# Layer with banded attention and eight routed experts: the first expert's last slots listed on chip by 0/1 products, roots in pairs, shorter groups of products, and an earlier release of chunk 3's table writes

## The chip, the cores and the metric

One Trainium2 chip, one core. The metric is device microseconds of one execution; the kernel before is given as the median of three runs, and one more execution was profiled. TensorE (PE) does the matrix products, VectorE (DVE) and ScalarE (ACT) work on what they leave in PSUM, GpSimd (POOL) does elementwise work and issues indirect DMAs (gathers, scatters), SyncE (SP) issues the plain DMAs. Each engine runs its own queue strictly in order.

## The reference, cut to what matters

2048 tokens of 512 numbers, 32 heads of 16, a band of 256 keys, and 8 experts of inner width 1376 of which each token takes two.

```python
def _A_ref(x, wqkv, wo):
    qkv = (x @ wqkv).reshape(B, S, 3, H, Dh).transpose(2, 0, 3, 1, 4)
    scores = jnp.einsum("bhqd,bhkd->bhqk", q, k) * (Dh ** -0.5)
    scores = jnp.where(mask, scores, -1e9)          # 0 <= query - key < 256
    o = jnp.einsum("bhqk,bhkd->bhqd", softmax(scores), v)
    return o.transpose(0, 2, 1, 3).reshape(B, S, D) @ wo

def _B_ref(x, wg, w1, w2):
    gates = _softmax(xt @ wg)
    topk_idx = jnp.argsort(-gates, -1)[:, :2]       # two experts per token, weights renormalised
    h = _gelu(jnp.einsum("nd,edf->nef", xt, w1))
    y = jnp.einsum("nef,efd->ned", h, w2)
    return jnp.einsum("ne,ned->nd", cw, y)

h = x + _A_ref(_layernorm(x), A_wqkv, A_wo)
return h + _B_ref(_layernorm(h), B_wg, B_w1, B_w2)
```

## The kernel before, in words

All products are made of three reduced-precision products, (high, high), (high, low), (low, high), so each operand is first split into two parts: ACT writes the high part, DVE or POOL subtracts to get the low one (`split`, L474).

The tokens go through attention in four chunks of 512 (chunk index c = 0 to 3, the fourth called the last here). A chunk has eight units of four heads; unit u = 8c + g. A unit's queries and keys go through DRAM into a layout of their own, `maxes` takes row maxima, and `attend` (L757) works on key tiles A, B, C, D: scores on PE, mask, exponential on ACT, then the product with V into the one PSUM tile `oT` (L835), four such V products for each unit of the last chunk. From unit 29 on (`LATE_MASKS`) the mask is put on the scores by DVE (L755) instead of POOL. ACT copies `oT` to `o_sb` (L850) and SP writes it to DRAM.

`project(c)` (L860) reads a chunk's attention output back (`fill`), multiplies by the inverse row sums (`part`, L905 on DVE or L903 on POOL), splits, and multiplies by the output weights (L913, twelve products of 512 columns for each block of 128 tokens). For the last chunk the inner dimension comes in three steps: heads 0 to 15 (k = 0, 1), 16 to 23 (k = 2), and 24 to 31 (k = 3), the last with its reciprocals on DVE (L947). Then come row statistics (L972), the root on POOL (`rstd`, L483, one call for each block), the normalisation (L988), the write of the normalised rows to DRAM (`xnd`), transposes on PE (L998), a copy by ACT (L1000) into the single buffer `nt_t`, and the gate products (L1005).

`route` (L1016) picks two experts for each token, finds each token's slot in its expert's list by a running count (products with 0/1 matrices, L1071 to L1076), and POOL scatters (token number, gate weight) into a DRAM `table`, one indirect DMA for each block and choice (L1102): eight for chunk index 2, eight for the last chunk in two lots of four. The eight of chunk index 2 each wait for one of the V products of units 29 and 30.

`experts` (L1172) runs eight experts. The first is expert number 0, whose slots 0 to 383 (three tiles, "early") can only hold tokens of the first three chunks, since the last chunk's tokens are put from slot 384 on (`EARLY`). Its table rows come in two reads: early ones after chunk index 2's scatters, the last two tiles (slots 384 to 597, "late") after all scatters. Token rows are gathered by POOL (L1316), transposed on PE (L1321), split; the up products are L1348 (12 in one task: 384 columns for the early tiles, 214 for the late ones), the activation L1356/L1362, the down products L1380 (33 for each tile of 128 tokens), the scaling L1391, and the result is added to the output by an indirect DMA (L1403). The other experts are taken in order of size, which `rank_experts` finds after all routing; weights come by L1209 (w1) and L1211 (w2).

The order on each engine is fixed when the kernel is built: every piece of work is a task with a priority, and a planner (`Plan.order`) simulates the engines with its own durations, giving each engine the ready task of lowest priority number. So the diff changes tasks, their dependencies and priorities, and the order of instructions follows from that.

## Time and profile before

| | us |
|---|---|
| three runs | 1045.19, 1047.86, 1051.26 |
| median | 1047.86 |
| the profiled execution, its own time | 1044.5 |
| its span, first to last instruction | 1042.4 |
| PE busy in the span | 1016.8 (98%) |

The profile page gives busy time for each engine and the share of the span; a timeline lists merged stretches of one engine with the start, the length, the line, the operation with its tiles, the count, and in brackets the idle time before it with what ended it. A windows view gives for each stretch its length, then busy time and count of PE, PEld (weight loads), DVE, ACT and POOL, then the granted TensorE clock as a share of 2.4 GHz, the DMA share and GB/s.

### The profile page before, as it was taken

How to read it: one execution, taken by the hardware profiler on the slowest of the kernel's cores; microseconds unless marked ns; L12 is line 12 of the kernel's file. 1: busy time of each engine (PE TensorE's matmuls, PEld its weight loads, DVE VectorE, ACT ScalarE, POOL GpSimd, SP SyncE). 2: the span in 40 equal slices, each digit the busy share in tenths (PEclk: the TensorE clock that was granted, in tenths of full speed). 3: DMA queues.
4: the chain of work that ended last, by engine and by line, in shares of the span. 5: the costliest groups of instructions: out<-in, count | busy, mean ns of one | idle time of the engine just before them, and what ended most of it. 6: DMA issues, size and time to landing. Idle time of an engine off the chain costs nothing. (4 is left out here: it accounts for less than half of the span.)

```text
span 1042.4 us, 19919 instructions
## 1 busy us (share of the span) xinstructions
PE 1016.8 (98%) x6722; PEld 842.0 (81%) x6722; DVE 645.6 (62%) x1951; ACT 536.9 (52%) x1143; POOL 623.3 (60%) x986
## 2 busy tenths in 40 slices
PE   8999999999999999998898999999999999999997
PEld 5877777877777777754887898998999989878795
DVE  8888876887677777787752556345453554544440
ACT  3487747575766656577631555163462543525340
POOL 5687749777887958758495144186483763834111
PEclk9999999999999999999998999999999999999999
DMA  6999877768696978764516344264444544454522
GB/s 214 291 249 240 250 190 214 224 179 202 191 251 164 200 159 210 201 167 110 190 49 148 97 141 113 63 153 111 115 97 128 157 94 105 123 139 151 124 77 29
DMA packets 143887, 164.48 MB, mean 158 GB/s; under 512 B 68587, under 2 KB 86571, under 8 KB 143776
## 3 DMA queue, kind: packets, MB, share of 16 engines
q1 hardware_dynamic: 128448, 145.96, 50.3%
q0 software_dynamic: 15328, 17.16, 9.9%
q8 instruction: 55, 0.90, 0.4%
q14 instruction: 56, 0.46, 0.2%
HBM read 111.10 MB, written 51.43 MB: 156 GB/s over the span
## 5 line engine op out<-in xcount | busy, mean ns | idle before, releaser
L735 DVE CUSTOM_DVE_ANT_0 one<-one,masked 128x320 f32<-128x320 f32 (+4 forms) x512 | 230.3, 494 | 57.9 <-PE one L730 55.0
L1348 PE MATMUL one<-mr 128*128 128x288 f32 (+14 forms) x1716 | 255.9, 310 | 1.3 <-ACT mr L476 0.7
L1348 PEld LDWEIGHTS one<-mr 128*128 128x128 f32 (+1 forms) x1716 | 244.5, 187 | 10.1 <-ACT mr L476 0.9
L785 ACT ACTIVATE zone<-one 128x384 f32<-128x384 f32 (+1 forms) x480 | 208.6, 495 | 80.1 <-PE one L779 60.6
L811 POOL TENSOR_SCALAR_AFFINE_SELECT zone<-zone 128x256 f32<-128x256 f32 (+1 forms) x332 | 151.1, 479 | 61.2 <-ACT zone L785 59.4
L1380 PE MATMUL one<-zone,mr 128*128 128x512 f32 (+4 forms) x648 | 154.9, 394 | 0.0
L480 POOL TENSOR_TENSOR mr<-mf,mr 128x512 fp32r<-128x512 f32 (+4 forms) x99 | 123.8, 1262 | 41.7 <-ACT mr L476 39.9
L1380 PEld LDWEIGHTS one<-zone,mr 128*128 128x128 f32 (+4 forms) x648 | 117.0, 182 | 31.4
L779 PE MATMUL one<-mr 98*128 98x384 f32 (+1 forms) x592 | 138.5, 327 | 3.1 <-ACT zone L785 1.9
L476 ACT CAST mr<-mf 128x512 fp32r<-128x512 f32 (+6 forms) x152 | 108.3, 734 | 46.0 <-DMA mf<-in_A_wqk_dram 15.3
L779 PEld LDWEIGHTS one<-mr 98*128 98x128 f32 x592 | 96.0, 190 | 42.9 <-ACT zone L785 14.1
L730 PE MATMUL one<-mr 96*128 96x320 f32 (+4 forms) x512 | 122.8, 315 | 1.5 <-DVE mx L735 0.9
L1287 POOL DMA_INDIRECT mf<-xnd,mf x94 | 106.4, 1132 | 28.8 <-issue 26.9
L1403 POOL DMA_INDIRECT out_dram<-mf,tb x24 | 41.5, 1730 | 130.6 <-DVE mf L1391 116.4
L478 DVE TENSOR_TENSOR mr<-one,mr 128x512 fp32r<-128x512 f32 (+16 forms) x161 | 79.1, 509 | 58.3 <-ACT mr L476 58.0
L1362 ACT ACTIVATE one<-one 128x288 f32<-128x288 f32 (+13 forms) x132 | 54.7, 415 | 104.1 <-PE one L1348 103.2
L661 PE MATMUL one<-mr 128*128 128x512 f32 (+1 forms) x396 | 103.7, 389 | 3.0 <-ACT mr L476 2.8
L730 PEld LDWEIGHTS one<-mr 96*128 96x128 f32 x512 | 87.7, 190 | 22.2 <-DVE mx L735 11.6
L1403 POOL DMA_INDIRECT out_dram<-mf x40 | 65.9, 1648 | 65.6 <-DVE mf L1433 57.1
L835 PE MATMUL oT<-zone 128*17 128x384 f32 (+2 forms) x1408 | 95.7, 389 | 0.1
L476 ACT CAST mr<-one 128x512 fp32r<-128x512 f32 (+16 forms) x161 | 70.6, 448 | 31.5 <-PE one L1321 17.3
L476 ACT CAST zone<-mf 128x512 fp32r<-128x512 f32 x72 | 42.1, 620 | 78.0 <-PE one L1423 48.5
(189 smaller groups left out, 1282.9 us busy)
## 6 DMA issues: line engine op xcount, KB each, us to landing
mf<-in_B_w_dram SPq DMA_DIRECT2D x32, 688.0 KB
mf<-in_B_w_dram SPq DMA_DIRECT2D x40, 512.0 KB
qkd<-mr SPq DMA_DIRECT2D x29, 512.0 KB
mr<-qkd SPq DMA_DIRECT2D x128, 96.0 KB
mr<-qkd SPq DMA_DIRECT2D x32, 384.0 KB
mf<-in_A_x_dram SPq DMA_DIRECT2D x32, 256.0 KB
mf<-in_A_wqk_dram SPq DMA_DIRECT2D x32, 256.0 KB
qkd<-mr SPq DMA_DIRECT2D x64, 128.0 KB
```

Of the source, the lines that this page charges most:

```text
L476: a = add("ACT", 51 + n * 0.86, lambda: nc.scalar.copy(dst_h(), src()), deps, prio, bufs)
L480: b = add("POOL", 60 + n * 2.3, lambda: nc.gpsimd.tensor_sub(dst_l(), src(), f32(dst_h())), [a], prio, bufs)
L661: nc.tensor.matmul(single[bk.h][:, s], wt()[:, int(i == 1), k * 128:(k + 1) * 128], xt[:, k, s], start=(i == 0 and k == 0), stop=(i == 2 a ...
L730: nc.tensor.matmul(view()[:, j], q_of(slot)[0:96, h + j, b].rearrange("p e q -> p (e q)"), K[slot.h][0:96, h + j, (b + k0) * 64:(b + 5) * ...
L735: nc.vector.tensor_tensor_reduce(v, v, masked[:, 320 - n:], scale=1.0, scalar=NEG, op0=OP.add, op1=OP.max, accum_out=mx_t[slot.h][:, h + j ...
L779: nc.tensor.matmul(single[bk.h][:, off:off + w], K[slot.h][0:98, h // 2, r * 128:(r + 1) * 128], q_of(slot)[0:98, h // 2, 2 * b:2 * b + 2 ...
L785: return add("ACT", 51 + n * 0.833, lambda: nc.scalar.activation(dst(), single[bk.h][:, 0:n].rearrange(order, **({"e": 2, "q": 64} if "e" ...
L811: nc.gpsimd.affine_select(v, v, pattern=[[0, v.shape[1]], [-1 if far else 1, 128]], compare_op=OP.is_gt if far else OP.is_ge, fill=0.0, ba ...
L1287: nc.gpsimd.indirect_dma_start(out=xg_t[i][:, t * 128:(t + 1) * 128], out_offset=None, in_=xnd4, in_offset=bass.IndirectOffsetOnAxis(ap=ql ...
L1348: nc.tensor.matmul(bank(), a[:, k, f * 128:f * 128 + w], spot[b][:, k, c0:c1], start=(i == 0), stop=(i == 11))
L1380: nc.tensor.matmul(single[bk.h][:n], h[a][:w], spot["w2"][2 * f + b][:w], start=(f == 0 and q == 0), stop=(f == NF - 1 and q == 2))
L1403: d = nc.gpsimd.indirect_dma_start(in_offset=None, compute_op=OP.add, **kw)
```

## The change

Seven edits, all between the last units of attention and the end of the first expert.

1. The first expert's table rows are read once, all five tiles, before the last chunk's scatters; the late tiles' entries are then only those of the earlier chunks. For the last chunk, DVE compares each token's slot number with a row of numbers 385 to 640 (`find`, 0/1 matrix of 128 tokens by 256 slots for each block), and PE multiplies these by (token number, weight) (`pick_late`, L1156, four products of two columns for each pair of blocks). DVE merges the result with the read rows (`merge`, L1536 to L1538), and the late tiles are gathered from that.
2. The scatters of the last chunk now wait for that read; the second lot of four waits for the late gathers. The ranking of the experts waits for the merge.
3. The eight scatters of chunk index 2 wait for V products of units 28 and 29.
4. The last chunk's roots are taken for two blocks at a time, and the copies of the transposed rows alternate between two buffers (`nt2`).
5. The first expert's up products are three tasks of four instead of one of twelve, and its down products one task for each 128 of the inner width instead of four tasks.
6. The low parts of the first expert's w2 are all made by DVE (before: POOL from f = 3 on).
7. In `part`, a block's split waits (in the plan) for the previous step's split of the same block; the k = 2 and k = 3 reads are planned after the use of the k = 0, 1 buffers.

```diff
+F0_PRIO, X0 = 8.0 * NC + 8.0, -8.2
...
-            ins = fill(3, o3, s3, 0, 512, last, last, p - 0.3, slot)
+            ins = fill(3, o3, s3, 0, 512, last + before_, last + before_, p - 0.3, slot)
...
+                if b % 2:
+                    b0 = b - 1
+                    root = rstd(lambda b0=b0: mv_t[0][:, b0:b0 + 2, 1], lambda b0=b0: ry_t[0][:, b0:b0 + 2], seen[-2:], pb + 0.4, 2)
...
-            tb, bk = Buf("nt"), Buf("one")
+            tb, bk = Buf("nt2" if end and b % 2 else "nt"), Buf("one")
...
+        def find():
+            pos = single[bk.h][:, 0:nb * E].rearrange("p (b e) -> p b e", e=E)
+            Vv.tensor_add(t["u"], pos, over(e_pos))
+            Vv.scalar_tensor_tensor(late_v[:, b0:b0 + nb], t["u"][:, :, 0], 1.0, t["m"][:, :, 0], op0=OP.add, op1=OP.mult)
+            for b in range(nb):
+                Vv.tensor_scalar(late_p[b], late_no, late_v[:, b0 + b:b0 + b + 1], None, op0=OP.is_equal)
+
+        def pick_late():
+            ps = single[hot[1].h][:, 0:4].rearrange("p (i q) -> p i q", q=2)
+            for b in range(nb):
+                for i in range(2):
+                    nc.tensor.matmul(ps[:, i], late_p[b][:, i * 128:(i + 1) * 128], late_r[:, b0 + b], start=(b0 + b + i == 0), stop=(b0 + b == 3),
+                                     skip_group_check=True)
...
-        for t, run in zip(route_done[NC - 2], pv_runs[8 * NC - 3] + pv_runs[8 * NC - 2]):
+        for t, run in zip(route_done[NC - 2], pv_runs[8 * NC - 4] + pv_runs[8 * NC - 3]):
...
-                                 src, dd, lo="POOL" if e == 0 and f >= 3 else "DVE"))
+                                 src, dd))
...
-            a = add("POOL", 950, g, [looked] + place, prio - 1.5, extra=2600)
+            a = add("POOL", 950, g, [looked] + place + (all_xn if e == 0 and not early else []), prio - 1.5, extra=2600)
             if e == 0 and not early:
                 late_rows.append(a)
+                for t in route_done[NC - 1][4:]:
+                    plan.after(t, [a])
...
+                    for i, (a, b) in enumerate(((w1h, "xh"), (w1l, "xh"), (w1h, "xl"))):
+                        def mm4(i=i, a=a, b=b, c0=c0, c1=c1, bank=bank):
...
-            for f0, f1 in ((0, 4), (4, 8), (8, 10), (10, NF)):
+            for f0, f1 in [(f, f + 1) for f in range(NF)] if e == 0 else ((0, 4), (4, 8), (8, 10), (10, NF)):
...
-                f1 = fetch(0, b - 8, all_routes + all_xn, EARLY // 128, nt)
+                f0 = fetch(0, F0_PRIO, sum((route_done[c] for c in range(NC - 1)), []) + [xn_done[i] for i in range(4 * NC - 4)], 0, nt)
+                for t in route_done[NC - 1]:
+                    plan.after(t, [f0])
+                old = add("DVE", 100, lambda: nc.vector.tensor_copy(late_t, tb0[:, :, 0]), [f0] + hot[:1], b - 10)
+
+                def merge():
+                    ps = single[hot[1].h][:, 0:4].rearrange("p (i q) -> p i q", q=2)
+                    nc.vector.tensor_tensor(late_t, late_t, ps[:, :, 0], op=OP.max)
+                    nc.vector.tensor_copy(tb0[:, :, 0], late_t)
+                    nc.vector.tensor_add(tb0.bitcast(F32)[:, :, 1], tb0.bitcast(F32)[:, :, 1], ps[:, :, 1])
+                f1 = add("DVE", 550, merge, [old] + hot[2:], 36, [hot[1]])
+                plan.after(sort, [f1])
```

What the planner makes of it is shown at three places. The first is PE's queue at the end of attention; the rows of `oT` with 17x128 and 17x256 that are the last of their kind are unit 31's last V product, the rows on `ident` are the transposes of the early token tiles, and `one_75`, `one_74` or `one_77`, `one_78`, `one_80` hold the four blocks' output projection. Before:

```order
L835 MATMUL oT<-zone 17x128 x4
L835 MATMUL oT<-zone 17x256 x4
L1321 MATMUL one_79<-ident,mf 128x128 x4
L1321 MATMUL one_74<-ident,mf 128x128 x4
L913 MATMUL one_75<-mr 128x512 x3
L913 MATMUL one_77<-mr 128x512 x3
L913 MATMUL one_80<-mr 128x512 x3
L913 MATMUL one_78<-mr 128x512 x3
L1321 MATMUL one_76<-ident,mf 128x128 x4
L1348 MATMUL one_79<-mr 128x384 x12
L1348 MATMUL one_74<-mr 128x384 x12
L913 MATMUL one_75<-mr 128x512 x2
```

And the same place in the changed kernel's queue of PE, where L841, L1385, L925 and L1424 are the lines that were L835, L1321, L913 and L1348:

```order
L925 MATMUL one_78<-mr 128x512 x3
L925 MATMUL one_80<-mr 128x512 x3
L1385 MATMUL one_76<-ident,mf 128x128 x4
L841 MATMUL oT<-zone 17x128 x4
L841 MATMUL oT<-zone 17x256 x4
L1424 MATMUL one_77<-mr 128x384 x12
L1424 MATMUL one_79<-mr 128x384 x12
L1424 MATMUL one_76<-mr 128x384 x12
L1424 MATMUL one_77<-mr 128x384 x12
L1424 MATMUL one_79<-mr 128x384 x12
L1424 MATMUL one_76<-mr 128x384 x8
L925 MATMUL one_75<-mr 128x512 x2
```

The three transposes and the twelve k = 2 products stand ahead of the last V product now, and between that and the first k = 3 product there are 68 up products where there were 24 up products and everything else.

The second place is PE's queue from the down products to the late tiles' up products. Before (L1266 is a lookup product for the second expert, the tiles with 128x86 and the 128x128 before it are the late ones, the next two are the second expert's):

```order
L1380 MATMUL one_77<-zone_5885,mr 128x512 x12
L1266 MATMUL one_74<-rm,pick 128x20 x2
L1321 MATMUL one_76<-ident,mf 128x128 x4
L1380 MATMUL one_77<-zone_5885,mr 128x512 x3
L1380 MATMUL one_77<-mr 128x512 x3
L1321 MATMUL one_75<-ident,mf 128x86 x4
L1321 MATMUL one_78<-ident,mf 128x128 x4
L1380 MATMUL one_77<-mr 128x512 x3
L1321 MATMUL one_80<-ident,mf 128x128 x4
L1348 MATMUL one_79<-mr 128x214 x12
```

In the changed kernel, where L1156 is the new product of the 0/1 matrices and L1455 the down products:

```order
L1455 MATMUL one_78<-zone_5928,mr 128x512 x12
L1156 MATMUL one_77<-mf 128x2 x4
L1455 MATMUL one_78<-zone_5928,mr 128x512 x12
L1455 MATMUL one_78<-mr 128x512 x6
L1455 MATMUL one_80<-zone_5928,mr 128x512 x6
L1385 MATMUL one_79<-ident,mf 128x128 x4
L1385 MATMUL one_76<-ident,mf 128x86 x4
L1455 MATMUL one_80<-zone_5928,mr 128x512 x12
L1424 MATMUL one_75<-mr 128x214 x12
```

Between the second list product and the late transposes stand 24 down products; 15 down products of the third early tile are left for after the late tiles' up products, as are the second expert's transposes.

The third place is POOL's queue around the late gathers, of which the second has 86 rows. Before, all scatters (L1102) come first:

```order
L1102 DMA table<-ent_6257,si_6290 18432x2
L1101 MEMSET spacer 1x1
L1102 DMA table<-ent_6257,si_6290 18432x2
L480 TENSOR_TENSOR mr<-mf,mr 128x384 x2
L480 TENSOR_TENSOR mr<-mf,mr 96x384
L1316 DMA mf<-xnd,tb_147 128x512
L1316 DMA mf<-xnd,tb_147 86x512
L1316 DMA mf<-xnd,tb_148 128x512 x3
```

In the changed kernel (L1161 the scatters, L1478 the adding of an early tile's result to the output, L1380 the gathers):

```order
L1161 DMA table<-ent_6200,si_6249 18432x2
L1130 COPY ent_6298<-tok 128x2 x2
L1477 MEMSET spacer 1x1
L1478 DMA out_dram<-mf,tb_147 1664x512
L1380 DMA mf<-xnd,tb_147 128x512
L1380 DMA mf<-xnd,tb_147 86x512
L1160 MEMSET spacer 1x1
L1161 DMA table<-ent_6298,si_6339 18432x2
```

The late gathers have moved ahead of the second lot of scatters and stand right behind the first early tile's result.

## Rows read from the trace of the kernel before

**Rows 1.** The profile page: busy time of each engine in the span, its share, and its instructions.
```profile
PE 1016.8 (98%) x6722; PEld 842.0 (81%) x6722; DVE 645.6 (62%) x1951; ACT 536.9 (52%) x1143; POOL 623.3 (60%) x986
```

**Rows 2.** Windows of 10 us: stretch, its length, then busy time (and count) of PE, PEld, DVE, ACT, POOL, the granted clock, DMA share, GB/s.
```profile
470.00:480.00 10.00, 9.45 (x70) 4.79 (x62) 7.72 (x27) 6.87 (x15) 9.16 (x17) 1.00 0.29 92
480.00:490.00 10.00, 9.64 (x73) 5.97 (x71) 7.09 (x26) 8.57 (x19) 7.28 (x8) 1.00 0.53 134
490.00:500.00 10.00, 5.93 (x41) 3.93 (x42) 6.95 (x11) 4.47 (x11) 6.22 (x5) 0.87 0.52 142
500.00:510.00 10.00, 9.32 (x49) 8.56 (x49) 6.41 (x15) 5.28 (x11) 1.75 (x2) 0.96 0.48 151
530.00:540.00 10.00, 10.00 (x60) 8.73 (x60) 5.64 (x29) 2.98 (x8) 9.19 (x17) 1.00 0.03 1
550.00:560.00 10.00, 8.66 (x41) 6.79 (x39) 3.02 (x8) 0.59 (x1) 7.04 (x7) 1.00 0.82 243
560.00:570.00 10.00, 7.21 (x37) 6.75 (x37) 1.29 (x3) 1.12 (x3) 5.37 (x7) 0.66 0.71 123
```

**Rows 3.** Timeline of PE from the last units of attention to the first expert's up products: start, length, line, tiles, count, idle before and what ended it.
```profile
478.32 1.10 PE L913 MATMUL one<-mr 128*128 128x512 f32 x4
479.26 0.92 PE L779 MATMUL one<-mr 98*128 98x256 f32 x5
490.94 1.97 PE L835 MATMUL oT<-zone 128*17 128x384 f32 x24
494.80 0.72 PE L1321 MATMUL one<-ident,mf 128*128 128x128 f32 x4 [1.90 <-DMA mf<-xnd,tb]
497.61 1.10 PE L1321 MATMUL one<-ident,mf 128*128 128x128 f32 x4 [2.09 <-DVE mf L905]
507.90 0.62 PE L913 MATMUL one<-mr 128*128 128x512 f32 x2
508.36 2.25 PE L1348 MATMUL one<-mr 128*128 128x384 f32 x12
510.45 1.08 PE L913 MATMUL one<-mr 128*128 128x512 f32 x4
```

**Rows 4.** Windows of 2 us where the granted clock is below 1.00; columns as in Rows 2.
```profile
498.00:500.00 2.00, 2.00 (x8) 1.71 (x7) 1.36 (x3) 0.89 (x2) 0.03 (x1) 0.50 0.60 174
500.00:502.00 2.00, 2.00 (x8) 1.59 (x8) 0.65 (x3) 0.30 (x1) 0.00 (x0) 0.81 0.82 193
...
562.00:564.00 2.00, 1.19 (x7) 1.15 (x8) 0.00 (x0) 0.30 (x1) 1.03 (x2) 0.55 0.99 220
564.00:566.00 2.00, 2.00 (x8) 1.60 (x7) 0.57 (x2) 0.14 (x1) 1.05 (x2) 0.50 0.81 143
566.00:568.00 2.00, 2.00 (x12) 2.00 (x11) 0.70 (x1) 0.00 (x0) 1.01 (x1) 0.50 0.28 75
```

**Rows 5.** Timeline of PE from the down products of the early tiles to the late tiles' up products; columns as in Rows 3.
```profile
537.75 12.10 PE L1380 MATMUL one<-zone,mr 128*128 128x512 f32 x51
557.88 0.75 PE L1321 MATMUL one<-ident,mf 128*128 128x128 f32 x4 [1.34 <-DMA mf<-xnd,tb]
562.81 1.76 PE L1321 MATMUL one<-ident,mf 86*128 86x86 f32 x8 [2.79 <-DMA mf<-xnd,tb]
566.36 16.11 PE L1348 MATMUL one<-mr 128*128 128x214 f32 x132
```

**Rows 6.** Timelines of POOL and of SP's queue: the first gather of an early tile, the last scatter, the table reads, the first two gathers (the late tiles), the loads of the second expert's w1.
```profile
491.31 1.00 POOL L1316 DMA_INDIRECT mf<-xnd,tb  x1 [1.49 <-DMA tb<-table]
...
544.53 0.96 POOL L1102 DMA_INDIRECT table<-ent,si  x1 [0.22 <-issue]
548.78 1.04 SPq L1243 DMA_DIRECT2D tb<-table  x2
551.04 0.98 SPq L1209 DMA_DIRECT2D mf<-in_B_w_dram  x2
551.33 0.99 POOL L1316 DMA_INDIRECT mf<-xnd,tb  x1 [2.64 <-DMA tb<-table]
552.62 1.46 POOL L1316 DMA_INDIRECT mf<-xnd,tb  x1 [0.30 <-issue]
```

**Rows 7.** Timelines of ACT, SP's queue and DVE behind the last V product: the copy of `oT`, the first of the two reads of what is written of it, the first reciprocal, the first product with it, and ACT's casts of the weights that stand among the projection's.
```profile
492.95 0.59 ACT L850 COPY zone<-oT 128x512 f32<-128x512 f32 x1 [0.93 <-PE oT L835]
497.82 0.52 SPq L887 DMA_DIRECT2D mf<-od  x1
504.22 2.57 DVE L947 RECIPROCAL mf<-mf 128x128 f32<-128x128 f32 x3
506.70 0.23 DVE L905 TENSOR_TENSOR mf<-mf 128x128 f32<-128x128 f32 x1
509.09 2.18 ACT L476 CAST zone<-mf 128x512 fp32r<-128x512 f32 x4
```

**Rows 8.** Timelines of DVE and POOL: the four k = 2 products with the inverse sums, what POOL does beside them, and three of the k = 3 ones.
```profile
493.29 4.30 DVE L905 TENSOR_TENSOR mf<-mf 128x128 f32<-128x128 f32 x4 [1.80 <-DMA mf<-od]
493.60 3.23 POOL L480 TENSOR_TENSOR mr<-mf,mr 128x688 fp32r<-128x688 f32 x2
507.70 1.01 DVE L905 TENSOR_TENSOR mf<-mf 128x128 f32<-128x128 f32 x3
```

**Rows 9.** Groups of instructions by line and shape from 470 to 585 us: the gate products, the narrow ones nearest to the new ones; columns are busy time, mean ns of one, idle before.
```profile
L1005 PE MATMUL one<-wgt,mf 128*128 128x8 f32 x32 | 3.8, 246 | 0.0
```

More of the change, by code (lines that the diff above doesn't have):

```diff
@@ L854, in layer @@
     scatter_i, last_fill = [], []
+    hot = []
     route_done = {}
@@ L896, in project, with part @@
         acc = {}
-        def part(b, k0, k1, o, s, deps, prio, bufs, start, stop, slow):
+        turns = {}
+        def part(b, k0, k1, o, s, deps, prio, bufs, start, stop, slow, used=None):
             n = (k1 - k0) * 128
@@ L1008, in project, with numbers, number_rows @@
         o_free[c], p2_end[c] = projs, projs + gates
+        if end:
+            def numbers():
+                nc.gpsimd.iota(late_no.bitcast(I32), pattern=[[1, 256]], base=EARLY + 1, channel_multiplier=0)
+            def number_rows():
+                nc.vector.tensor_copy(late_no, late_no.bitcast(I32))
+                nc.vector.tensor_copy(late_r[:, :, 0], tok[:, 4 * c:4 * c + 4])
+            hot.append(add("DVE", 500, number_rows, [add("POOL", 400, numbers, projs, p + 1.5)], p + 1.5))
         route_done[c] = []
```

79 lines of the change are left out of this document (61 added, 18 removed).

## The prediction

> **What bounds the kernel now.** I read the page first: PE is busy for 1016.8 of 1042.4 us, so all that an edit off PE can give back is PE's idle time and the time that it runs at a lower clock [rows 1]. Then windows of 10 us through the stretch that the diff touches, which show where that time lies: PE is idle for 0.55, 0.36, 4.07 and 0.68 us in the four from 470 to 510, and for 1.34 and 2.79 us in the two from 550 to 570; from 510 to 550 it is full [rows 2]. PE's own timeline names what ended each gap. Behind the last V product, which ends at 492.91, it waits 1.90 and 2.09 us at the transposes of early token tiles; the first wait ends with the gather's landing [rows 3]. At the late tiles it waits 1.34 and 2.79 us for their gathers [rows 5]. Idle time is followed by a low clock: the 2 us windows from 498 on and from 562 on show a granted clock down to 0.50, that is 1.2 GHz instead of 2.4. Busy time times the missing share of the clock gives 1.00 + 0.38 there, and 0.54 + 1.00 + 1.00 here, 3.9 us in all [rows 4]. So the stretch holds 9.8 us of idle time and 3.9 us of slow running, 13.7 us, and no edit here can give more.
>
> **The late tiles (edits 1, 2).** Before, the chain is: the last scatter begins at 544.53, the table read is issued at 548.78, the gathers at 551.33 and 552.62, and PE uses them at 557.88 and 562.81, 6.5 and 10.2 us after their starts [rows 5, 6]. The first early gather was used 3.5 us after its start (491.31 to 494.80) [rows 3, 6]; the late ones share the DMA engines with the loads of the second expert's w1, issued at 551.04 [rows 6]. The change takes scatters, landing and table read out of this chain. Call P the end of PE's second list product. DVE's merge is three tiny operations, I take 0.9 us with the hops (estimate from the 0.23 us of a 128-column one [rows 7]), so the gathers start at P + 1.1 and, 1.3 later, P + 2.4, and are usable 3.5 us on at P + 4.6 and P + 5.9. PE has 24 down products meanwhile, at 12.10/51 = 0.237 us each 5.7 us [rows 5], and then the first transposes, some 0.7. I take a remaining wait of 0.5 us, with 0 and 6.4 us as bounds (the second gather as slow as before: P + 12.6 against P + 6.2). The w1 loads come after the expert ranking, which is queued on DVE behind the merge, so by then the gathers should be in. What is gained here is 4.13 us of idle and the 2.5 us of slow running behind it, less 0.5.
>
> The new work on PE is eight products of two columns. The gate products, 32 with eight columns, took 3.8 us, 0.119 each [rows 9], so I add 0.95 us. DVE's comparisons, its eight more low parts of w2, and the merge lie beside the down products: DVE is busy for 5.64 of 10 us there [rows 2]. If that cover were gone, they would delay the list product, which stands in PE's queue behind 15 down products of cover, 3.6 us.
>
> The second expert's table read moves behind the second lot of scatters. Four scatters of 1.3 us after the gathers end at P + 8.7, the read follows 3.3 later (544.53 + 0.96 to 548.78) and lands 2.6 later (548.78 to 551.33) [rows 6], P + 14.6. PE wants its lookup product seven groups of late up products on: P + 5.7 + 1.4 + 12 × 0.237 + 7 × 12 × 0.122 = P + 20 [rows 5]. So that is hidden, with about 4 us to spare after DVE's part.
>
> **The end of attention (edits 3, 5, 7).** The scatters of chunk index 2 come about a unit earlier, and the table read with them, so the early tiles are there before attention ends and the two gather waits at 494.80 and 497.61 go, with most of the other 1.59 us of idle and the 1.4 us of slow running. Their transposes (3 × 0.65) and the twelve k = 2 products (four take 0.94 us from start to start, so 2.8 [rows 3]) now stand ahead of the last V product. PE does 4.8 us more before it, less the idle filled, so that I expect it to end near 497 to 499.
>
> What is late next is the path that this product starts, and that is the main cost I see. Before, the first k = 3 product runs at 507.90 without a wait, 15.0 us after the last V product [rows 3]. Its operand path is: copy of `oT` at 492.95, write, reads at 497.82, reciprocals at 504.22, first product with them at 506.70, then ACT's cast [rows 7]; it can be ready some 0.5 us before PE came, 14.5 us after the V product (estimate from these rows). In the changed order PE has only 68 up products to do meanwhile. Twelve take 2.09 us from start to start (508.36 to 510.45 [rows 3]), so 68 take 11.8, and PE waits 14.5 - 11.8 = 2.7 us; the bounds are 0 (the reads land sooner, with less beside them) and 4. The other k = 3 operands pass through ACT among casts of weights (four took 2.18 us [rows 7]) and PE has only four up products between them, so that I add either 1.5 us of further short waits or a fall of the clock as in [rows 4], 1 to 2.5 us. I take 2.0 for the two.
>
> On DVE the four k = 2 products with the inverse sums now stand ahead of the masks of unit 31's last scores, and PE's queue ends in the V product that needs these. The four took 4.30 us beside two POOL subtractions of 1.6 us, where three of the same kind took 1.01 us alone [rows 8]. So they cost 1.3 to 4.3 us on DVE, in front of the last exponentials, with about 2 us of cover in PE's queue; I take a wait of 1.0 (0 to 2.3). The Trainium skill, "SBUF — State Buffer", section "Who interferes with whom", says that a DVE instruction with two SBUF inputs and a GpSimd instruction that reads SBUF exclude each other for the whole instruction; [rows 8] agree with it. By that rule the wait would be nearer to 2.3, and the sum 1.3 us smaller. For one more short fall of the clock in the crowded queue of units 30 and 31 I take 0.7.
>
> The earlier scatters themselves cost nothing on POOL: they are the same eight, and POOL's queue had a gap there; one of them now precedes a few masks of unit 28, 1 us, which can cost PE 0 to 0.5 and is in the 0.7. Roots in pairs and the second copy buffer only shorten the routing path, which PE's up and down products cover; I put them at 0.
>
> **The sum.** 13.7 - 0.95 (list products) - 0.5 (late gathers) - 2.7 - 2.0 (k = 3) - 1.0 (k = 2 on DVE) - 0.7 leaves 5.85; 0.5 us comes back because the clock also recovers in the window after 568, which [rows 4] leave out. So the profiled execution would go from 1044.5 to about 1038.1 (span 1036.0), and the median of 1047.86, which lies 3.4 above that execution, to 1041.5: 6.4 us less, 0.6%. A measurement of this kernel can tell about 0.5%, 5.2 us, from no change.
>
> **Rivals.**
> (a) Nothing new waits: the read-back lands early and the clock stays at 2.4 GHz through the end of attention. For it: the k = 3 path was never waited for before. Then 2.7, 2.0 and most of 1.7 come back, a gain of 11, 1037. Against: the 14.5 us rest on rows and the 68 products on the order.
> (b) The end of attention gives back what it saved: the V product comes at 501 or later because DVE's products run into POOL, PE waits 4 us at k = 3, and the clock falls twice. Then that part gains nothing, and the late tiles alone give 4.13 + 2.5 - 0.95 - 0.5 less 2 to 3 of new slow running: 2.5 us, 1045.4, no change.
> (c) Slower: the late gathers collide with transfers again. Their place is PE's transposes 24 down products behind the list product; the price is 6.4 us of idle instead of 0.5 and 3 us of slow running behind it, so 6.4 + 0.5 - 6.4 - 3.0 = -2.5, 1050.4; with (b) at the end of attention, 1054. It decides from about 8 us between a gather's start and its use. For it: 6.5 and 10.2 us before. The Trainium skill, "DMA: Bandwidth & Descriptors", section "Issuing engines are not separate DMA queues", says that transfers from all issuing engines run on the same 16 DMA engines and interleave; the late gathers beside the w1 loads agree. Against: the first early tile's result is all that is queued just ahead, and the w1 loads wait for the ranking.
> (d) The change doesn't do what it says: the late gathers stand on POOL behind the first early tile's addition to the output, which waits for 33 down products and DVE's scaling. If that slips by 5 us, the gathers come as late as before relative to PE, and 4.13 + 2.5 stay lost: 1048, no change.
>
> **How the numbers follow.** Forecast, 1038 to 1044: 0.52, of which 0.42 gain over 5.2 us. (a) 0.12. (b) 0.20. (c) 0.10. (d) 0.06, half of it a little slower than 0.5% if the added work comes on top. So faster 0.54, within 0.5% 0.10 + 0.20 + 0.03 = 0.33, slower 0.13. The range leaves out the better half of (a) and most of (c): 1036 to 1049.
>
> **What would show it.** In the changed profile PE's transposes at the late tiles should show no wait above 1 us and the late gathers' use some 3.5 to 5 us after their start; the early transposes should lie before the last V product; that product should end at 497 to 499; and the first k = 3 product should show a wait of 2 to 3 us, with a granted clock near 0.5 behind it. If that wait is absent, (a) holds; if DVE's k = 2 products take 4 us and the last V product ends after 501, (b). Wrong altogether would be a new wait in the second expert (its lookup product, its w1), which I have at nothing.

## The result and the profile after

The changed kernel takes 1054.36 us in the median of 13 runs (1048.82 to 1058.91), the kernel before 1047.68 in 13 runs beside it (1042.26 to 1052.63): a ratio of 1.0067, 95% interval 1.0051 to 1.0083. It is slower by 6.7 us where 6.4 us less was forecast. The profiled execution took 1055.76 us with a span of 1054.0 (before: 1042.4) and a mean granted clock of 0.981, at the low end of the 13 executions (0.981 to 0.990), so this profile shows more slow running than most. Some 2.9 us of that difference stand ahead of the change: unit 27's first V product begins at 439.86 before and at 442.80 after, in a queue that the change has not touched up to there.

The page after, engine busy times (before: [rows 1]):
```profile
PE 1025.2 (97%) x6738; PEld 846.8 (80%) x6738; DVE 651.6 (62%) x1977; ACT 536.8 (51%) x1143; POOL 613.4 (58%) x971
```

The span is 11.6 us longer: PE has 16 instructions more and is busy 8.4 us longer, and it is idle 3.2 us longer. Windows of 10 us of the changed kernel show where; columns are the stretch, its length, PE busy (count), the granted clock, DMA share, GB/s (before from 470 on: [rows 2]):
```profile
450.00:460.00 10.00, 8.86 (x76) 1.00 0.64 143
460.00:470.00 10.00, 7.29 (x35) 0.57 0.62 174
470.00:480.00 10.00, 9.84 (x47) 0.50 0.18 52
480.00:490.00 10.00, 9.86 (x55) 0.91 0.28 66
490.00:500.00 10.00, 9.01 (x74) 1.00 0.64 222
500.00:510.00 10.00, 7.92 (x39) 0.83 0.12 44
560.00:570.00 10.00, 4.37 (x20) 0.86 0.78 177
570.00:580.00 10.00, 10.00 (x65) 0.80 0.51 102
```
The first two of these in the kernel before:
```profile
450.00:460.00 10.00, 8.76 (x75) 0.99 0.56 135
460.00:470.00 10.00, 8.95 (x54) 0.84 0.49 177
```

The idle time did not grow much: over 450 to 510 and 560 to 580 it is 12.85 us after; before, from 450 to 510 and 550 to 570, 12.08. The slow running did: busy time times the missing share of the clock is 12.9 us after (3.13 + 4.92 + 0.89 + 1.35 + 0.61 + 2.00), and 5.1 before. PE stood at 1.2 GHz from some 461 to 481, in units 29 and 30. Two places differ from the forecast.

The late tiles, timelines of PE, POOL and SP's queue (before: [rows 5, 6]):
```profile
546.65 0.95 PE L1156 MATMUL one<-mf 128*128 128x2 f32 x8
555.42 0.95 PE L1156 MATMUL one<-mf 128*128 128x2 f32 x8
557.54 1.02 POOL L1380 DMA_INDIRECT mf<-xnd,tb  x1 [2.03 <-issue]
558.86 1.46 POOL L1380 DMA_INDIRECT mf<-xnd,tb  x1 [0.30 <-issue]
560.42 0.98 SPq L1273 DMA_DIRECT2D mf<-in_B_w_dram  x2
561.88 0.63 PE L1385 MATMUL one<-ident,mf 128*128 128x128 f32 x4
568.13 0.85 PE L1385 MATMUL one<-ident,mf 86*128 86x86 f32 x4 [5.63 <-DMA mf<-xnd,tb]
568.71 5.42 PE L1455 MATMUL one<-zone,mr 128*128 128x512 f32 x12
```
P, the end of the second list product, is 556.37. The gathers start at P + 1.2 and P + 2.5, as forecast. The first is used without a wait. The second is used 9.3 us after its start; PE waits 5.63 us, and the twelve down products behind it take 5.42 us at the low clock.

The end of attention, PE's timeline, then SP's queue (before: [rows 3, 7]):
```profile
460.64 0.44 PE L785 MATMUL one<-mr 98*128 98x384 f32 x1 [1.47 <-issue]
466.60 0.69 PE L785 MATMUL one<-mr 98*128 98x384 f32 x1 [0.77 <-ACT zone L791]
498.64 0.84 PE L841 MATMUL oT<-zone 128*17 128x256 f32 x16 [0.99 <-ACT zone L856]
504.29 0.73 PE L925 MATMUL one<-mr 128*128 128x512 f32 x2 [1.19 <-ACT mr L482]
510.67 0.84 PE L841 MATMUL oT<-zone 128*17 128x128 f32 x16
511.44 12.07 PE L1424 MATMUL one<-mr 128*128 128x384 f32 x68
523.35 0.62 PE L925 MATMUL one<-mr 128*128 128x512 f32 x2
514.27 0.52 SPq L894 DMA_DIRECT2D mf<-od  x1
```
The early transposes wait for nothing now. But the last V product ends at 511.51 where 497 to 499 was forecast, and short waits (0.99, 1.19 and some smaller) stand in its way. The first k = 3 product, 11.8 us behind it, shows no wait at all.

### The profile page after: what moved, and what is told of

The parts are those of the page before. It is cut to its first block, busy times and chain, and to the rows that moved or that the text cites. A ratio compares the mean times of both kernels' runs of the same rounds, so it can differ in the third digit from the quotient of the medians.

```text
span 1054.0 us, 19958 instructions
## 1 busy us (share of the span) xinstructions
PE 1025.2 (97%) x6738; PEld 846.8 (80%) x6738; DVE 651.6 (62%) x1977; ACT 536.8 (51%) x1143; POOL 613.4 (58%) x971
## 5 line engine op out<-in xcount | busy, mean ns | idle before, releaser
L1414 PE MATMUL one<-mr 128*128 128x290 f32 (+15 forms) x1452 | 214.4, 309 | 0.0
L1414 PEld LDWEIGHTS one<-mr 128*128 128x128 f32 (+1 forms) x1452 | 205.9, 186 | 7.9
L1455 PE MATMUL one<-zone,mr 128*128 128x512 f32 (+4 forms) x648 | 157.8, 399 | 0.0
L785 PE MATMUL one<-mr 98*128 98x384 f32 (+1 forms) x592 | 142.3, 333 | 6.5 <-issue 3.5
L1455 PEld LDWEIGHTS one<-zone,mr 128*128 128x128 f32 (+4 forms) x648 | 118.6, 184 | 31.9
L785 PEld LDWEIGHTS one<-mr 98*128 98x128 f32 x592 | 98.2, 194 | 48.4 <-ACT zone L791 14.1
L482 ACT CAST mr<-mf 128x512 fp32r<-128x512 f32 (+6 forms) x152 | 108.2, 734 | 40.8 <-DMA mf<-in_B_w_dram 10.6
L484 DVE TENSOR_TENSOR mr<-one,mr 128x512 fp32r<-128x512 f32 (+16 forms) x161 | 79.6, 510 | 69.1 <-ACT mr L482 57.1
L1478 POOL DMA_INDIRECT out_dram<-mf,tb x24 | 41.5, 1730 | 128.6 <-DVE mf L1466 95.5
L1478 POOL DMA_INDIRECT out_dram<-mf x40 | 64.8, 1620 | 63.3 <-DVE mf L1508 54.8
L841 PE MATMUL oT<-zone 128*17 128x384 f32 (+2 forms) x1408 | 98.1, 397 | 1.0 <-ACT zone L856 1.0
```

What stands on the lines that cost most here:

```text
L482: a = add("ACT", 51 + n * 0.86, lambda: nc.scalar.copy(dst_h(), src()), deps, prio, bufs)
L785: nc.tensor.matmul(single[bk.h][:, off:off + w], K[slot.h][0:98, h // 2, r * 128:(r + 1) * 128], q_of(slot)[0:98, h // 2, 2 * b:2 * b + 2 ...
L1414: nc.tensor.matmul(bank(), a[:, k, f * 128:f * 128 + w], spot[b][:, k, c0:c1], start=(i == 0), stop=(i == 11))
L1455: nc.tensor.matmul(single[bk.h][:n], h[a][:w], spot["w2"][2 * f + b][:w], start=(f == 0 and q == 0), stop=(f == NF - 1 and q == 2))
L1478: d = nc.gpsimd.indirect_dma_start(in_offset=None, compute_op=OP.add, **kw)
```

## The experiments

Each ratio is against runs of the kernel before on the same chip.

| kernel | median us | before | ratio | 95% interval |
|---|---|---|---|---|
| e1_waits_back | 1052.19 | 1043.40 | 1.0084 | 1.0064 to 1.0104 |
| e2_waits_only | 1052.42 | 1043.40 | 1.0078 | 1.0056 to 1.0100 |
| e3_loads_hold | 1045.69 | 1043.40 | 1.0028 | 1.0009 to 1.0047 |
| e4_both | 1046.97 | 1043.40 | 1.0030 | 1.0014 to 1.0046 |
| e5_hold_128 | 1047.82 | 1046.86 | 1.0009 | 0.9992 to 1.0026 |
| e6_both_128 | 1048.72 | 1046.86 | 1.0027 | 1.0006 to 1.0048 |
| e7_before_128 | 1044.26 | 1046.86 | 0.9964 | 0.9946 to 0.9982 |
| e8_after_128 | 1048.00 | 1046.86 | 1.0006 | 0.9983 to 1.0028 |
| e9_before_128_waits | 1059.27 | 1048.90 | 1.0095 | 1.0068 to 1.0123 |
| e10_after_128_waits_back | 1049.54 | 1048.90 | 1.0007 | 0.9987 to 1.0026 |
| e11_after_96, one run | 1050.64 | 1048.90 | | |
| e12_after_88, one run | 1045.68 | 1048.90 | | |
| e13_after_128_later | 1051.44 | 1043.68 | 1.0076 | 1.0062 to 1.0089 |
| e14_before_128_later | 1060.64 | 1043.68 | 1.0166 | 1.0152 to 1.0179 |
| e15_after_128_roots | 1042.29 | 1043.68 | 0.9981 | 0.9960 to 1.0002 |
| e16_waits_back_roots | 1042.74 | 1043.68 | 0.9995 | 0.9978 to 1.0011 |

### The table writes and the loads, first round

Theory A was that edit 3, the earlier table writes, costs the end of attention; its rival B was that the multiplications that moved cost it. For the late tiles, theory C was a collision with the w1 loads, and theory D the adding store ahead of the gathers on the same queue. e1 is the changed kernel with this line back:
```diff
-        for t, run in zip(route_done[NC - 2], pv_runs[8 * NC - 4] + pv_runs[8 * NC - 3]):
+        for t, run in zip(route_done[NC - 2], pv_runs[8 * NC - 3] + pv_runs[8 * NC - 2]):
```


> The changed kernel with one edit undone: chunk 3's table writes wait for the V products of units 29 and 30 again, so a write no longer stands on POOL ahead of unit 28's last masks, and six of the eight stand behind the casts of w1. Everything else of the change stays. Theory A (the earlier table writes cost the end of attention: TensorE waits for masks and roots around 458 to 467 and then runs at half clock to 481): the stretch at a granted clock of 0.50 is as short as in the kernel before (under 5 us instead of 20), the last V product ends 5 to 8 us earlier than in the changed kernel, and the time falls by 5 to 7 us, to 0.999 to 1.003 of the kernel before. Theory B (the multiplications, reciprocals and transposes that moved cost it): the half-clock stretch stays and the time stays at 1.005 to 1.008. In both, the wait at the second late tile (5.6 us) stays.

e2 is the kernel before with the line of the change.

> The kernel before with only that one edit: the table writes wait for the V products of units 28 and 29. Theory A: the end of attention shows what the changed kernel shows, six table writes in a row on POOL, TensorE waits at 458 to 467 and a half-clock stretch of over 10 us behind them; 4 to 7 us slower, ratio 1.004 to 1.007, although the first gathers start some 3 us earlier. Theory B: no such stretch, ratio 0.997 to 1.001. In both, the late tiles wait as in the kernel before.

e3 is the changed kernel with
```diff
-                late_rows.append(a)
+                late_rows.append(dma(lambda: nc.sync.dma_start(rd[0][j:j + 1, 0:1], xg_t[j][0:1, 0:1]), 64, [a], prio - 1.0))
```


> The changed kernel with the second expert's first two w1 loads held back until both late gathers have landed (SP copies one number of each gathered tile to a scratch row ahead of them, and so waits for the gathers). No other engine's order changes. Theory C (the two loads of 688 KB, issued 1.6 and 2.9 us after the gathers, share the DMA engines with them): the second late tile lands 4 to 5 us after its gather started instead of 9.3, TensorE's wait there falls from 5.6 us to under 1.5, the clock behind it stays at 1.00, and the time falls by 5 to 7 us, to 0.999 to 1.002. Theory D (the gathers stand behind the adding store of the first early tile, 3.7 us ahead of them on the same queue, and cost what they cost): the gather still takes 8 to 9 us, the wait stays, and the ratio stays at 1.005 to 1.008.

> Both edits on the changed kernel: table writes behind units 29 and 30 as in the kernel before, and the loads held until the late gathers have landed. If A and C both hold, the gains add, 11 to 13 us against the changed kernel and 4 to 7 us against the kernel before, ratio 0.993 to 0.997. If only A or only C holds, 0.999 to 1.003. If neither, 1.005 to 1.008.

e1 did not get faster. Its profile lost only 1.7 us to a low clock in units 29 and 30 (counted as in the table of missing clock below), but with a mean clock of 0.992 it is the best of its six executions (0.984 to 0.992). The waits at the early tiles came back, 2.66 and 1.80 us in the windows 490 to 510, and 4.66 us stayed at the second late tile. e2 got slower as A said and shows A's low clock (8.6 us lost in the same place), but also a wait of 9.35 us at the late tiles that A had not named. So A failed one test and passed the other only in part. e3 took some 4 us off the changed kernel (1.0067 to 1.0028), where C asked for 5 to 7, and e4 stood where one theory alone should have put it. Why not more, e3's timelines of POOL and PE and its 1 us windows (columns as above) show:
```profile
548.55 1.01 POOL L1380 DMA_INDIRECT mf<-xnd,tb  x1 [2.03 <-issue]
549.87 1.45 POOL L1380 DMA_INDIRECT mf<-xnd,tb  x1 [0.31 <-issue]
552.89 0.63 PE L1385 MATMUL one<-ident,mf 128*128 128x128 f32 x4
556.87 0.71 PE L1385 MATMUL one<-ident,mf 86*128 86x86 f32 x4 [3.34 <-DMA mf<-xnd,tb]
```
```profile
550.00:551.00 1.00, 1.00 (x6) 1.00 0.62 135
551.00:552.00 1.00, 1.00 (x6) 1.00 0.33 127
552.00:553.00 1.00, 1.00 (x6) 1.00 0.27 27
553.00:554.00 1.00, 0.53 (x5) 1.00 0.17 54
554.00:555.00 1.00, 0.00 (x0) 1.00 0.15 54
```
With no load in the way the second gather still took 7.0 us, and near its end the DMA engines were 0.15 to 0.17 busy, which is two to three of sixteen. No load competes, only table writes run beside it: few engines carry the gather. Its packets, counted in e5's expectation below, pass two at a time. In e4, where the adding store comes behind the gathers, it took 7.26 us, so D is out too.

### 86 rows or 128

The late gathers differ in their rows: the first has 128, the second 86. e5 to e8 gather 128 rows for that tile (the 42 more are spare rows that nothing uses) in e3, e4, the kernel before and the changed kernel:
```diff
-            bk = Buf("one")
+            bk, g_n = Buf("one"), 128 if e == 0 else w
...
-                nc.gpsimd.indirect_dma_start(out=xg_t[j][:w], out_offset=None, in_=rows(xnd, e, i),
-                                             in_offset=bass.IndirectOffsetOnAxis(ap=tb_t[e][:w, i, 0:1], axis=0))
+                nc.gpsimd.indirect_dma_start(out=xg_t[j][:g_n], out_offset=None, in_=rows(xnd, e, i),
+                                             in_offset=bass.IndirectOffsetOnAxis(ap=tb_t[e][:g_n, i, 0:1], axis=0))
```


> With the loads held, the second late gather still took 7.0 us from its start (549.87) to its use (556.87), and TensorE waited 3.34 us. That gather lists 86 rows, every other early or late one 128. In the records its packets of 4 KB come one every 80 ns or so, two at a time, from 551.6 to 556.2, while the 64 packets of the gather ahead of it passed in under 1 us. This kernel is that one, but the last late tile gathers 128 rows (rows 86 to 127 point to spare rows, and nothing uses them). Theory E (a gather of 86 rows is spread over two DMA engines, one of 128 over all sixteen): the second gather lands within 4.5 us, the wait at the second late tile falls from 3.34 to under 0.7 us, no fall of the clock behind it, 3 to 4.5 us faster than with the held loads alone, ratio to the kernel before 0.998 to 1.000. Theory F (its rows are slow for another reason, such as the table writes behind it on the same queue): 128 rows take as long or longer, the wait stays at 3 to 4 us, ratio 1.002 to 1.004.

> The same 128 rows in the kernel with both edits (table writes behind units 29 and 30, loads held), whose second late gather took 7.26 us from start to use with a wait of 2.89 us. Theory E: the wait goes, 2.5 to 4 us faster than with both edits, ratio 0.998 to 1.000 of the kernel before. Theory F: ratio 1.002 to 1.004, as with both edits.

> The kernel before with only the gather of 128 rows in place of 86 for the last late tile; no engine's order changes. There the two late gathers took 6.6 us (551.33 to 557.88) and 10.2 us (552.62 to 562.81) beside two w1 loads, with waits of 1.34 and 2.79 us and half clock to 566. Theory E: the second gather lands with or soon after the first, its wait of 2.79 us falls to under 1 and the clock behind it stays up, 2.5 to 5 us faster, ratio 0.995 to 0.998. If the loads alone make the second gather late (theory C alone): no change, 0.999 to 1.001.

> The changed kernel with only the gather of 128 rows, the two w1 loads not held. Its second late gather took 9.3 us with a wait of 5.63. If 86 rows cost about 3 us of it and the loads 2.3 (theories C and E together): wait 1.5 to 3, ratio 1.003 to 1.005 of the kernel before. If the loads alone set it: wait 5 to 6 us, ratio 1.006 to 1.008. If the rows alone set it: wait under 1, ratio 0.999 to 1.001.

The wait at the second late tile is gone in all three kernels of the change, in e8 too, where the loads still run beside the gathers. e8, timelines of POOL, SP's queue and PE:
```profile
557.16 0.95 POOL L1380 DMA_INDIRECT mf<-xnd,tb  x1 [0.30 <-issue]
558.72 0.98 SPq L1273 DMA_DIRECT2D mf<-in_B_w_dram  x2
560.17 1.44 PE L1385 MATMUL one<-ident,mf 128*128 128x128 f32 x8
```
And e5, windows of 1 us after its second gather (start 552.80), without loads:
```profile
553.00:554.00 1.00, 1.00 (x6) 1.00 0.67 164
554.00:555.00 1.00, 1.00 (x6) 1.00 0.67 156
555.00:556.00 1.00, 1.00 (x7) 1.00 0.54 206
```
More rows are over sooner: share 0.67 where e3 has 0.15. In e8 the transposes of both late tiles run in one stretch, 3.0 us after the second gather's start, and the ratio falls from 1.0067 to 1.0006, some 6 us. That the rows alone set the wait was the last of e8's three cases (wait under 1, 0.999 to 1.001). The loads, first suspect in the prediction and in theory C, cost the gather of 86 rows 2.3 us (9.3 beside them, 7.0 without); behind a gather of 128 rows they cost nothing that PE sees, and e5, with the loads held as well, is no better than e8. The kernel before gains from the same edit: 0.9964, the lowest ratio of all that was run, though e15's interval below overlaps it.

In the kernel before the loads start ahead of the gathers, and there a gather of 128 rows is late too. e7, timelines of SP's queue, POOL and PE:
```profile
558.40 0.98 SPq L1209 DMA_DIRECT2D mf<-in_B_w_dram  x2
558.69 0.99 POOL L1316 DMA_INDIRECT mf<-xnd,tb  x1 [2.03 <-DMA tb<-table]
566.21 0.75 PE L1321 MATMUL one<-ident,mf 128*128 128x128 f32 x4 [1.69 <-issue]
```
The first late tile, 128 rows, is used 7.5 us after its gather's start. No run holds these loads back there, so their share of the 7.5 us is not shown.

e11 and e12 look at the row count, 96 and 88 in place of 128 (`-(-w // 32) * 32` and `-(-w // 8) * 8`).

> The changed kernel with 96 rows in the last late gather. If the rows are dealt over as many DMA engines as divide their number evenly (86 rows over two, 96 and 128 over sixteen): no wait over 0.7 us at the second late tile, as with 128. If a gather under 128 rows is slow as such: a wait of 4 to 6 us, as with 86.

> The same with 88 rows. If the rows are dealt over as many DMA engines as divide their number evenly, 88 rows go over eight (11 each) and land within about 1 us of what 96 rows take: a wait under 1 us. If only a multiple of 16 is dealt out and all else goes over two or so: a wait of 4 to 6 us, as with 86.

Neither waits at the second late tile. The second gather and the transposes of both late tiles in e11's timelines, then in e12's:
```profile
559.51 0.94 POOL L1380 DMA_INDIRECT mf<-xnd,tb  x1 [0.30 <-issue]
562.53 1.08 PE L1385 MATMUL one<-ident,mf 128*128 128x128 f32 x8
```
```profile
554.31 1.00 POOL L1380 DMA_INDIRECT mf<-xnd,tb  x1 [0.30 <-issue]
557.33 1.30 PE L1385 MATMUL one<-ident,mf 128*128 128x128 f32 x8
```
Two rows more, 88, and the gather is quick: its transposes come some 3 us after its start and wait for nothing, where 7.0 to 9.3 went by with 86. By the traces' packet records the second gather's packets take 1.2 us in e11 and in e12, 4.3 in e3 and 6.0 in the changed kernel. So a gather under 128 rows is not slow as such. 86 is twice a prime number, and of the numbers up to 16 only 1 and 2 divide it; 88, 96 and 128 have large divisors there. The Trainium skill, "DMA: Bandwidth & Descriptors", section "Why a DMA increments its semaphore by 16 and not by 1", states this as a rule: a DMA is dealt over the largest number of engines, up to 16, that divides the outer sizes of both sides. By it 86 rows would go over 2 engines, 88 over 11, 96 and 128 over 16. The trace agrees: share 0.15 to 0.17 of sixteen engines with 86 rows, some table writes among them, and 0.67 with 128. The runs do not tell this rule from a coarser one, such as a multiple of 8: only 86, 88, 96 and 128 rows were run.

### The square: earlier waits, and the rest

With quick gathers in both kernels, the change still is 4.4 us behind (1.0006 against 0.9964). e9 is e7 with the earlier waits alone, e10 is e8 with the old waits; they ran on another chip than e7 and e8, each pair beside the kernel before.

> The kernel before with the gather of 128 rows and, of the change, only the earlier waits of the table writes (V products of units 28 and 29). With the kernel before with 128 rows (0.9964) and the changed kernel with 128 rows (1.0006) it makes two sides of a square whose late tiles wait for nothing long. Theory A (of the 4.4 us that the changed kernel is still behind, the earlier waits of the table writes cost most, by short waits and half clock in units 29 and 30): 0.999 to 1.002. Theory G (the rest of the change costs it: the list's products, the merged rows, the split groups): 0.995 to 0.998.

> The changed kernel with the gather of 128 rows and the table writes waiting for units 29 and 30 again: the fourth corner of that square. Theory A: 0.995 to 0.998, as good as the kernel before with 128 rows. Theory G: 0.999 to 1.002, as the changed kernel with 128 rows.

| with 128 rows | waits on units 29, 30 | waits on units 28, 29 |
|---|---|---|
| list from the table (before) | 0.9964 | 1.0095 |
| list on chip and the rest | 1.0007 | 1.0006 |

Neither theory gives this. The earlier waits cost 1.3% in one row and nothing in the other; the rest of the change costs 0.4% in one column and gives back 0.9% in the other. e9's timelines of POOL and PE show the first:
```profile
557.31 1.64 POOL L1403 DMA_INDIRECT out_dram<-mf,tb  x1 [2.44 <-DVE mf L1391]
559.41 1.57 POOL L1403 DMA_INDIRECT out_dram<-mf,tb  x1 [0.43 <-DVE rf L1258]
561.29 1.02 POOL L1316 DMA_INDIRECT mf<-xnd,tb  x1 [0.30 <-issue]
567.55 2.73 PE L1321 MATMUL one<-ident,mf 128*128 128x128 f32 x12 [6.75 <-DMA mf<-xnd,tb]
```
With the earlier waits the planner puts the transposes and k = 2 products ahead of the last V product, which ends at 504.40 here; routing of the last chunk is later for it, and the late gathers stand on POOL behind two early tiles' additions to the output. In e7 the late gathers start at 558.69 in an execution that is 4.0 us later at unit 27, and PE waits 1.69 us. So in e9 the late tiles pay for the early ones: 6.75 us of waiting and a clock of 0.68 and 0.63 in the windows 560 to 580. The list on chip makes that chain shorter, and this is what it buys in the changed kernel. Without the delay it has nothing to buy, and costs: in e10 PE's timeline has the list products (1.9 us) and new waits ahead of normalised rows, of the list and of the late tiles' split:
```profile
523.81 1.28 PE L1029 MATMUL one<-ident,mf 128*128 128x128 f32 x8 [0.98 <-DVE mf L1009]
547.88 0.61 PE L1156 MATMUL one<-mf 128*128 128x2 f32 x4 [0.51 <-DVE mf L1150]
560.26 5.01 PE L1424 MATMUL one<-mr 128*128 128x214 f32 x28 [2.34 <-ACT mr L482]
```
1.9 + 0.98 + 0.51 + 2.34, less e7's 1.69, makes 4.0 us, near the 4.5 between e10 and e7, but it is no account of them, since e7 waits elsewhere. From 440 to 590 PE is idle for 10.6 us in e10's trace and for 10.9 in e7's; what differs is slow running, 12.4 us against 5.2. Over all executions e10's mean granted clock stands lower against the kernel before than e7's by 0.0027 (95% interval 0.0005 to 0.0049), which is up to 2.8 us of a span. So the list's 1.9 us of products are certain, and more than half of the 4.5 us may be lower clock.

### A third point, and the roots

e13 and e14 put `pv_runs[8 * NC - 2] + pv_runs[8 * NC - 1]` into e8 and e7. e15 and e16 take one root for each block again, in e8 and e10:
```diff
-                if b % 2:
-                    b0 = b - 1
-                    root = rstd(lambda b0=b0: mv_t[0][:, b0:b0 + 2, 1], lambda b0=b0: ry_t[0][:, b0:b0 + 2], seen[-2:], pb + 0.4, 2)
-                    for b1 in (b - 1, b):
+                if True:
+                    root = rstd(lambda b=b: mv_t[0][:, b, 1:2], lambda b=b: ry_t[0][:, b:b + 1], [a], pb + 0.4, 1)
+                    for b1 in (b,):
```


> The changed kernel with 128 rows, with the table writes of chunk 3 waiting for the V products of units 30 and 31: one unit later than in the kernel before, two later than in the change. If the table writes among the masks hold the 4.4 us (theory A), the half-clock stretch between 455 and 485 shrinks to under 7 us, against it stand the first tiles, whose rows come some 8 us later: 0.997 to 1.001. If the length of that stretch is chance (theory H: 3 to 17 us long in six traces of the same order), only the later rows count: waits of 4 to 8 us more around 500, 1.004 to 1.009.

> The kernel before with 128 rows and the same later waits. Theory A: 0.995 to 0.998, no slower than with units 29 and 30. Theory H: 1.000 to 1.005, slower by the later rows of the first tiles.

> The changed kernel with 128 rows, with one root for each row block of the last chunk again instead of one for two. If the pairs hold part of the 4.4 us (the first block of a pair waits for the second's statistics): 1 to 2 us faster, 0.998 to 1.000. If not: 1.000 to 1.002, since POOL has twice the root instructions on the way to the router.

> The same in the changed kernel with 128 rows and the table writes behind units 29 and 30. There TensorE waited 0.98 us at 523.81 for a normalisation. If the pairs hold part of it: 0.997 to 1.000. If not: 1.000 to 1.002, and what is left against the kernel before with 128 rows is the list's products (1.9 us) and the clock.

Later writes are worse in both kernels (1.0076, 1.0166): there PE waits more than 4 us near 500, at k = 2 products whose casts are not ready, ahead of which the early tiles' transposes stand in the kernel before, and in e14 7.26 us at the late tiles. That is theory H, and more than it asked for in e14. Single roots came out at 0.9981 and 0.9995, 2.6 and 1.3 us better than the pairs by the ratios, but these come from different chips and the intervals overlap; they point to a cost of the pairs of 1 to 3 us and don't prove it. A longer wait for the second block's statistics is not what they show: from 490 to 540 PE is idle for 3.1 us in e8's trace and in e15's, and for 4.6 and 4.1 in e10's and e16's.

The slow stretch in units 29 and 30 went where no theory sent it. Two traces, windows of 10 us, first e15 (earlier waits), then e16 (old waits):
```profile
460.00:470.00 10.00, 8.45 (x53) 0.97 0.65 187
470.00:480.00 10.00, 9.86 (x55) 0.86 0.17 36
```
```profile
460.00:470.00 10.00, 9.62 (x40) 0.56 0.46 160
470.00:480.00 10.00, 9.59 (x56) 0.75 0.09 28
```
The missing clock (sum of one minus the granted clock, times 10 us, over the three windows from 450 to 480), one profiled execution each:

| waits | us missing |
|---|---|
| units 28, 29 | after 9.3, e2 8.6, e3 1.7, e5 5.2, e8 8.2, e9 5.2, e11 7.1, e12 6.8, e15 1.7 |
| units 29, 30 | before 1.7, e1 1.7, e4 6.8, e6 8.5, e7 3.5, e10 8.6, e16 6.9 |
| units 30, 31 | e13 6.8, e14 6.8 |

Kernels of one line have the same order on each engine through the last units of attention (e5 to e16 have one small copy more at the start), and spread from 1.7 to 9. The means are 6.0, 5.4 and 6.8. With the writes taken from among the masks altogether (third line) it is no less. So the loss of 9.3 us in the changed kernel's trace against 1.7 before is mostly chance, in a stretch where all these traces show short waits of PE (of 0.2 to 1.5 us in the kernel before and the changed one); where the timeline names a cause it is an exponential on ACT or a row maximum on DVE.

One trace is one draw, but the granted clock of every execution is on record. In 23 executions of the kernel before on one chip its mean over the span goes from 0.987 to 0.999. The mean of all executions of a kernel, less that of the kernel before on the same chip, in thousandths; one thousandth is about 1 us of the span, less where PE is idle anyway:

| changed kernel with | waits on units 28, 29 | waits on units 29, 30 |
|---|---|---|
| loads held | e3 -2.3 | e4 -0.1 |
| loads held, 128 rows | e5 -0.7 | e6 -0.4 |
| 128 rows | e8 -3.3 | e10 0.0 |
| 128 rows, single roots | e15 -0.6 | e16 +2.0 |

The earlier waits stand lower in all four pairs, by 2.1 on average (95% interval 0.7 to 3.5). So beside the chance there is a cost of edit 3 in clock, some 2 us; these means don't say in which stretch. The ratios of the pairs differ by 0 to 0.2% the other way, so elsewhere edit 3 gives back as much or more.

## Why the prediction was wrong

**What bounds the kernel** was read rightly: the time moved with PE's idle and slow running, for the most part in the stretch (2.9 us of the two profiles' difference stood ahead of it).

**The late tiles** is the step that failed: "usable 3.5 us on at P + 4.6 and P + 5.9", with a remaining wait of 0.5 us. The starts were right to 0.1 us, the first tile right, the second was used at P + 11.8 and cost 5.63 us and some 2.6 of slow running. The 3.5 us came from a gather of 128 rows and was used for one of 86. The 10.2 us that the trace of before shows for that same gather [rows 5, 6] were put down to the w1 loads, which the change moves behind the gathers, so the clue was explained away. Nor were the gathers in when the loads came: these were issued at 560.42, 1.6 us after the second gather's start. What the runs show in its place: 7.0 us without any load, 9.3 beside them, and in the changed order no wait some 3 us after the start with 88, 96 or 128 rows, with the loads behind it or held. This term alone is 6 of the 13 us between forecast and result (e8). Rival (c) had the place and the price (6.4 and 3.0; with (b) 1054) and a cause, colliding transfers, that holds for 2.3 of the 9.3 us only; its "decides from about 8 us" fits 9.3. Another row of the same group spoke too: the 86-row gather occupied POOL for 1.46 us, the other for 0.99 [rows 6]; with 128 rows it takes 0.95.

**The products of the list** were put at 0.95 us; PE's timeline has twice that, 1.9, since each of the eight makes two instructions (16 more on the page). Mis-sized by 0.95.

**The end of attention.** The early transposes moved and their waits went, as forecast (the prediction counts both as waits for a gather; the row of before names a DVE product for the second, 2.09 us). The last V product, forecast for 497 to 499, ended at 511.51; in the best trace with the same order, e15, at 501.87, still 3 us late. Of the 9.6 us between these two, 2.8 stood ahead of unit 27 already, and the rest goes with the slow clock (9.3 us missing against 1.7). Rival (b) had this product at 501 or later, but through 4 us of DVE's products and 4 us of waiting at k = 3; the products took 2.8, and that wait did not come.

One more short fall of the clock was priced at 0.7 us. What the traces show for this queue is 5 to 6 us on average and 1.7 to 9.3 singly, before the change too, so one profile of before (1.7) gave a base that was too good; and edit 3 adds some 2 us by the clock of all executions. The 0.7 was too small. In all, edit 3 gave this part little: from unit 27's first V product to the first k = 3 product, less 0.174 us for each up product between, the nine traces with the earlier waits take 62.0 to 69.1 us (mean 65.5), the seven with the old waits 63.9 to 69.2 (mean 66.8).

**k = 3**: -2.7 and -2.0 did not come. SP's reads were issued 2.8 us after the V product's end (514.27) instead of 4.9, and the first product ran after 11.8 us without a wait. The lower bound of 0 was right, the value from the queue of before too high.

**k = 2 on DVE**, priced at 1.0: the four products take 2.82 us on DVE, within the 1.3 to 4.3 allowed. PE waits 1.19 us for the cast behind them at 504.29 and 0.51 at 505.54, 1.7 in all: somewhat more than the 1.0, and within its bounds.

**What was not in the prediction at all** is that the gains don't add. It gave edits 1 and 2 the late tiles' wait and edit 3 the early tiles' wait. But edit 3 alone delays routing so much that the late tiles wait longer (e9, 1.0095), and the list on chip uses its gain to undo that. With the gather mended the whole change stands at 1.0006, against 0.9964 for the kernel before mended in the same way. Of that 4.4 us the list's 1.9 us of products are certain. The mean clock is lower too, 0.9875 in e8 against 0.9936 in e7 on the same chip, which is up to 6 us of the span and more than is left. A cost of the pairs of roots, which the prediction put at 0, is likely and not proven; how these add up is open, and so is what remains of the 13 us between forecast and result beside the 6 of the late tiles.

## What to carry to other kernels

Read a transfer's duration from a row of the same shape: count its rows, and if the count has no large divisor up to 16, pad it; here the same edit is worth 0.4% before and 0.6% after the change. When two edits shorten two waits on one chain, time all four corners, since one may only be paying for the other. And before pricing a clock fall from one profile, see how much the same queue varies over several, and how the mean clock varies over all executions.

## What the runs showed that was not expected

A gather of 172 KB in 86 rows takes 7.0 us from start to use, one of 256 KB in 128 rows, also without loads (e5), is there when PE comes for it 3 us after its start, with DMA shares of 0.15 and 0.67 while they last. And the same instructions in the same order, with short waits among them, lost between 1.7 and 8.6 us to the half clock from one execution to another (the seven traces with the old waits).
